# Reordering the first expert's start, the weight conversions and the buffer pools of an attention, expert and gated-MLP kernel

## The chip, the cores and the metric

The kernel runs on one core of a Trainium2 chip. The metric is the time of one execution on the device in microseconds. The engines are TensorE (PE in the rows; PEld is its weight load), VectorE (DVE), ScalarE (ACT), GpSimd (POOL) and SyncE (SP), which issues most transfers.

## The reference

Three layers follow each other; all data are float32 except that the last three matrices are stored as float64 and are read as such by the kernel.

```python
# 1. linear attention: 4 batches, 8 heads, 576 tokens, 64 wide
kv  = einsum('bhsd,bhse->bhde', k, v)
out = einsum('bhsd,bhde->bhse', q, kv)
out = out / sqrt(mean(out * out, -1) + 1e-6) * g_norm      # -> x: 2304 tokens x 512
# 2. experts: 8 of them, each token goes to 2
logits = x @ w_gate + log1p(exp(x @ w_noise)) * noise
top2, weights = two largest, softmax over the two
out[mask] += weight * (relu(x[mask] @ w1[e]) @ w2[e])      # w1 512x1024, w2 1024x512
# 3. gated MLP, 2304 tokens, 512 -> 1536 -> 512
gate = 1 / (1 + exp(-(x @ w_gate)))
out  = (gate * (x @ w_val)) @ w_out
```

## The kernel before

Every product of float32 is made of three products of halves: a high half `h` that PE's number format holds and the low half `l` that is left (high by high, high by low, low by high). ScalarE makes a high half (`activation(hi, raw, Copy)`), VectorE the low half (a subtraction of `hi` from `raw`).

The work comes in stages. **Attention** runs over 18 token tiles of 128; `attend` writes rows to `xbuf` in HBM and `route(g)`, a generator that `advance` steps on, makes ranks and lists for four groups of tiles: its steps on VectorE give the mask `mk`, PE turns it into ranks `prk`, and VectorE makes one-hot rows `ohv`, from which PE makes the lists `lsa` (the first two blocks of expert 0) and `lsb` (all others). **Experts**: GpSimd gathers an expert's tokens by such a list (`gather`), the rows are scaled (`scale`: `xs`), turned on PE (`pxT`) and split into `xh` and `xl` (`expert_in`). Expert 0 starts on its first two blocks before all ranks are known: `h_first(fp, 0)` makes four products `ph`, 24 matmuls each, that `h_out` turns into `ha`; then come `y_step`s (`py`), the second part of expert 0, and experts 1 to 7, each with eight `h_step`s (`ph`, then `hh` on ScalarE and `hl` on VectorE) and five `y_step`s, whose rows go to `ybuf`. **The gated MLP** gathers each token's two rows (`fetch`: `yg`), scales and adds them (`combine`), turns them (`turn`: `px`), and makes the first two tiles in 12 units (`first_unit`: `pgv`) while the others are prepared (`x_parts`); the other 16 tiles take 84 products by a seven-product scheme, whose weight sums `ws` are made beforehand, and the output matrix ends it.

Weights come in units. `tasks` is a list of them in order: an expert's four parts of `w1` and of `w2`, and among them, from the 17th unit on, the parts of the three last matrices, one for every 2.8 units. `load_piece` loads the next raw part into one of four buffers as one comes free; `work` does the next task, and `pump(t)` after each PE step calls it as a planner's credit, free places and expected loads allow. A part of `wg`, `wv` or `wo` is turned from float64 in six VectorE instructions for each of its two halves (`from_double`). A `wo` part is stored to `obuf` and gives its place back; `wg` and `wv` are stored to `wbuf` and keep theirs until `first_weights` splits them in the gated stage. There are 28 places in all; a split part of an expert takes two.

The order on SP and GpSimd is that of the program throughout, on ScalarE nearly so, on VectorE from the second part of expert 0 on, on PE from the last down products on; elsewhere a scheduler orders by priority and its own estimate. `behind(x)` holds GpSimd's queue until `x` is written, by a copy to `seen`. PSUM has eight banks: `psP` has two buffers of two banks and `psA` four of one.

## Time and profile before

| | |
|---|---|
| runs | 953.31, 954.02, 956.75 us; median 954.02 |
| profiled execution | 954.98 us; span of its instructions 953.2 us |
| mean granted TensorE clock | 0.984 |
| busy | PE 919.9 us, PEld 795.6, DVE 690.0, ACT 439.1, POOL 380.9 |
| DMA | 213.93 MB, mean 224 GB/s |

Busy time is that in which an engine works on an instruction; the weight load overlaps the products. The granted clock is a share of full speed, 2.4 GHz; its two levels here are 1.0 and 0.5.

### The profile page before, as it was taken

The numbers are of one execution on the slowest core, as the hardware profiler recorded it, in microseconds if no ns is written. First come the engines' busy times: TensorE is split into PE (matmuls) and PEld (weight loads), VectorE is DVE, ScalarE is ACT, GpSimd is POOL, SyncE is SP. The second block draws the span as 40 slices with busy tenths as digits, with TensorE's granted clock in tenths as the row PEclk, the third lists the DMA queues.
The fourth block names the chain that finished last, engine by engine and source line by source line (L and its number), as shares of the span: only waits on it lengthen the run. The fifth ranks groups of instructions, "written<-read, shape, count | busy, mean of one in ns | idle before, by whom it ended". The sixth has DMA issues, their size and how long they took to land.

```text
span 953.2 us, 14355 instructions
## 1 busy us (share of the span) xinstructions
PE 919.9 (97%) x5155; PEld 795.6 (83%) x5155; DVE 690.0 (72%) x1033; ACT 439.1 (46%) x659; POOL 380.9 (40%) x369
## 2 busy tenths in 40 slices
PE   7987999999999999999999989999999999999998
PEld 4876889889897988979889889888788888888886
DVE  1488688859877595987876458897977876876463
ACT  1674354434343333343343657655555455554441
POOL 2141474737475473736600363242254636300000
PEclk8997999999999999999999989999999999999999
DMA  9995578868776365675753466798477767986784
GB/s 263 281 279 167 189 238 290 282 228 302 256 242 203 112 212 175 211 243 150 243 175 107 131 193 195 230 292 284 143 244 264 264 225 266 343 286 199 221 249 99
DMA packets 134380, 213.93 MB, mean 224 GB/s; under 512 B 20384, under 2 KB 65952, under 8 KB 134304
## 3 DMA queue, kind: packets, MB, share of 16 engines
q1 hardware_dynamic: 122128, 190.05, 61.5%
q0 software_dynamic: 7664, 20.26, 7.4%
q10 hardware_dynamic: 4512, 2.66, 1.0%
q8 instruction: 41, 0.67, 0.3%
q14 instruction: 35, 0.29, 0.1%
HBM read 140.94 MB, written 71.97 MB: 223 GB/s over the span
## 4 chain that ended last, share of the span: by engine, by line
PE 57%; DVE 8%; DMA 3%; issue 3%; ACT 1%; DVEq 0%; SPq 0%; ACTq 0%
PE pga L1163 12%; PE py L806 11%; PE poa L1342 7%; PE ph L762 6%; PE pgc L1163 6%; PE pgv L1131 4%; PE poc L1342 3%; PE pgb L1163 3%; PE pout L1312 2%; PE pob L1342 2%; DVE hl L768 1%; DMA raw<-in_moe_w_dram 1%; DVE raw L611 1%; DMA raw<-in_moe_w_val_dram 1%; ACT hh L767 1%
## 5 line engine op out<-in xcount | busy, mean ns | idle before, releaser
L703 POOL DMA_INDIRECT xg<-xbuf,lsq x132 | 152.4, 1154 | 55.9 <-issue 32.5
L983 DVE TENSOR_TENSOR wt<-lw,wt 128x512 fp32r<-128x512 f32 x84 | 70.9, 850 | 33.2 <-ACT wt L982 27.3
L767 ACT ACTIVATE hh<-ph 128x624 fp32r<-128x624 f32 (+1 forms) x60 | 41.6, 697 | 97.7 <-PE ph L762 74.1
L768 DVE SCALAR_TENSOR_TENSOR hl<-ph,hh 128x624 fp32r<-128x624 f32 (+1 forms) x60 | 48.7, 811 | 52.1 <-ACT hh L767 47.1
L703 POOL DMA_INDIRECT yg<-ybuf,slot x36 | 39.5, 1096 | 83.8 <-DMA ybuf<-yo 44.2
L752 ACT ACTIVATE xh<-xT 128x512 fp32r<-128x512 f32 (+3 forms) x40 | 21.1, 544 | 77.3 <-DVE xT L749 73.5
L722 POOL TENSOR_TENSOR xg<-xg 128x512 f32<-128x512 f32 x33 | 36.7, 1115 | 39.9 <-DMA xg<-xbuf,lsq 39.6
L982 ACT ACTIVATE wt<-lw 128x512 fp32r<-128x512 f32 x84 | 49.8, 621 | 0.3 <-DMA lw<-wbuf 0.2
L1200 POOL TENSOR_TENSOR qt<-qv 128x512 f32<-128x512 f32 x12 | 18.9, 1579 | 69.7 <-DVE qv L1187 27.7
L684 POOL COPY seen<-hh 128x1 f32<-128x1 f32 x42 | 19.4, 462 | 65.5 <-ACT hh L767 64.6
L1177 ACT ACTIVATE q<-pga 128x1024 f32<-128x1024 f32 x24 | 24.7, 1027 | 42.7 <-PE pga L1163 39.6
L811 ACT ACTIVATE yo<-py 128x512 f32<-128x512 f32 (+1 forms) x40 | 23.6, 591 | 42.9 <-PE py L806 37.4
L762 PE MATMUL ph<-xl,w_0h 128*128 128x312 f32 (+2 forms) x128 | 40.2, 314 | 2.4 <-DVE xl L753 2.4
L753 DVE TENSOR_TENSOR xl<-xT,xh 128x512 fp32r<-128x512 f32 (+3 forms) x40 | 25.2, 641 | 23.8 <-ACT xh L752 23.8
L1131 PE MATMUL pgv<-x0h,w 128*128 128x256 f32 x192 | 39.2, 297 | 3.3 <-issue 2.5
L762 PE MATMUL ph<-xh,w_0h 128*128 128x312 f32 (+2 forms) x128 | 40.2, 315 | 1.0 <-ACT xh L752 0.9
L762 PE MATMUL ph<-xh,w_2h 128*128 128x312 f32 (+2 forms) x128 | 39.7, 310 | 1.0 <-DVE hl L768 1.0
L762 PE MATMUL ph<-xh,w_0l 128*128 128x312 f32 (+2 forms) x128 | 39.8, 311 | 0.3 <-PEq L841 0.3
L762 PE MATMUL ph<-xh,w_3h 128*128 128x312 f32 (+2 forms) x128 | 39.3, 307 | 0.3 <-DVE hl L768 0.3
L762 PE MATMUL ph<-xh,w_3l 128*128 128x312 f32 (+2 forms) x128 | 39.3, 307 | 0.0
L762 PE MATMUL ph<-xh,w_1h 128*128 128x312 f32 (+2 forms) x128 | 39.3, 307 | 0.0
L762 PE MATMUL ph<-xh,w_2l 128*128 128x312 f32 (+2 forms) x128 | 39.2, 306 | 0.1
(559 smaller groups left out, 3134.1 us busy)
## 6 DMA issues: line engine op xcount, KB each, us to landing
raw<-in_moe_w_dram SPq DMA_DIRECT2D x60, 512.0 KB
lw<-wbuf SPq DMA_DIRECT2D x84, 256.0 KB
gr<-qbuf SPq DMA_DIRECT2D x42, 512.0 KB
ybuf<-yo SPq DMA_DIRECT2D x32, 256.0 KB
ybuf<-zero SPq DMA_DIRECT2D x29, 256.0 KB
raw<-in_moe_w_gate_dram SPq DMA_DIRECT2D x12, 512.0 KB
raw<-in_moe_w_val_dram SPq DMA_DIRECT2D x12, 512.0 KB
raw<-in_moe_w_out_dram SPq DMA_DIRECT2D x12, 512.0 KB
```

Of the source, the lines that this page charges most:

```text
L703: nc.gpsimd.indirect_dma_start(out=x, out_offset=None, in_=src, in_offset=bass.IndirectOffsetOnAxis(ap=ix, axis=0))
L722: eng.tensor_mul(xv, xv, x[:, :, 128:, None].to_broadcast([128, 4, KD, 32]))
L753: nc.vector.tensor_sub(XL[e, s][:, :, a:z], pt[:, :, o:o + z - a], XA[e, s][:, :, a:z].bitcast(FT))
L762: nc.tensor.matmul(ph, w[:, c, j], x[e, s][:, c, :], start=(n == 0), stop=(n == 3 * KD - 1))
L767: nc.scalar.activation(hh, ph, AF.Relu)
L768: nc.vector.scalar_tensor_tensor(hl, ph, 0.0, hh.bitcast(FT), op0=OP.max, op1=OP.subtract)
L806: nc.tensor.matmul(py[0:m], x[:, f % 2, t], w[:, f % 2, :], start=(n == 0), stop=(n == 3 * FC - 1))
L982: nc.scalar.activation(hi, src, AF.Copy)
L983: nc.vector.tensor_sub(lo, src, hi.bitcast(FT))
L1131: nc.tensor.matmul(pg[:, k // 2, 0:PC], w[:, a, d, s], X0[x][:, 2 * (k % 2) + d, :], start=(k % 2 == 0 and d + a + x == 0), stop=(k % 2 == ...
L1163: nc.tensor.matmul(ps[:, j, 0:HT[c]], w[:, a, k, s], x[:, k, :], start=(first and i == 0), stop=(i == 5), skip_group_check=not first)
L1342: nc.tensor.matmul(ps[:, j, 0:HT[c]], w, g[x][1][:, f, :], start=(first and u + f + i == 0), stop=(u == FP3 - 1 and f + i == 3), skip_grou ...
```

## The change

In the start of expert 0, `work(lows)` puts off the low halves of the first two `w1` parts, with the load behind each. After the scaling of the first two blocks comes the first low half, then the turning and splitting of the tokens, then the first product in three passes (high by high, low weights, low tokens) with steps of the ranks and the second low half between them; DVE and PE keep this order. One of two `advance` steps ahead of it moves behind it. In the task list the six parts of `wo` come first, then `wg` and `wv`, and the last down products pump conversions as others do. From expert 1 on the PSUM pools are made anew: three double-bank buffers for `ph`, two for `py`; a new pool's tile waits for the tiles whose space it takes. In the gated stage the gathers of tiles 5 to 9 go out one by one, each behind a unit's product, and combine, turn and the x parts are put to other steps; so are the gathers of tiles 10 to 13.

```diff
@@ -61,7 +61,7 @@
 PLACES = 11
-FETCHES = {10: 7, 11: 8, 12: 10, 13: 12, 14: 18, 15: 22, 16: 26, 17: 30}
+FETCHES = {10: 9, 11: 10, 12: 12, 13: 13, 14: 18, 15: 22, 16: 26, 17: 30}
 OUT_LOADS = 6
@@ -133,8 +133,9 @@
     gp = moe.enter_context(tc.tile_pool(name="gp", bufs=GBUFS))
-    psP = moe.enter_context(tc.tile_pool(name="psP", bufs=2, space=bass.MemoryType.PSUM))
-    psA = moe.enter_context(tc.tile_pool(name="psA", bufs=4, space=bass.MemoryType.PSUM))
+    banks = moe.enter_context(ExitStack())
+    psP = banks.enter_context(tc.tile_pool(name="psP", bufs=2, space=bass.MemoryType.PSUM))
+    psA = banks.enter_context(tc.tile_pool(name="psA", bufs=4, space=bass.MemoryType.PSUM))
 
@@ -560,7 +561,7 @@
         units += [("w1", e, i) for i in range(FP)] + [("w2", e, i) for i in range(FP)]
-    m2 = [(n, 0, i) for i in range(FP2) for n in ("wg", "wv")] + [("wo", 0, i) for i in range(FP2)]
+    m2 = [("wo", 0, i) for i in range(FP2)] + [(n, 0, i) for i in range(FP2) for n in ("wg", "wv")]
 
@@ -614,7 +615,7 @@
 
-    def work():
+    def work(lows=None):
 
@@ -629,13 +630,19 @@
             wst[u], places[u] = (hi, lo), (i, j)
-            if u[0] == "w1":
-                nc.scalar.activation(hi, raw, AF.Copy, scale=gcol)
-                nc.vector.scalar_tensor_tensor(lo, raw, gcol, hi.bitcast(FT), op0=OP.mult, op1=OP.subtract)
+            nc.scalar.activation(hi, raw, AF.Copy, **({"scale": gcol} if u[0] == "w1" else {}))
+
+            def low():
+                if u[0] == "w1":
+                    nc.vector.scalar_tensor_tensor(lo, raw, gcol, hi.bitcast(FT), op0=OP.mult, op1=OP.subtract)
+                else:
+                    nc.vector.tensor_sub(lo, raw, hi.bitcast(FT))
+                load_piece()
+
+            if lows is None:
+                low()
             else:
-                nc.scalar.activation(hi, raw, AF.Copy)
-                nc.vector.tensor_sub(lo, raw, hi.bitcast(FT))
-            load_piece()
+                lows.append(low)
         elif u[0] == "ws":
@@ -778,7 +785,7 @@
 
-    def h_first(fp, s):
+    def h_first(fp, s, between=None):
 
@@ -788,8 +795,17 @@
         ph = pp([128, 2, 512], "ph")
-        for j in range(2):
-            h_half(ph[:, j, 0:n], 0, 2 * fp + j, s)
+        if between:
+            hi, lo = wst["w1", 0, fp]
+            for k, (w, x) in enumerate(((hi, XA), (lo, XA), (hi, XL))):
+                for j in range(2):
+                    for c in range(KD):
+                        nc.tensor.matmul(ph[:, j, 0:n], w[:, c, j * 128:(j + 1) * 128], x[0, s][:, c, :],
+                                         start=(k + c == 0), stop=(k == 2 and c == KD - 1))
+                between(k)
+        else:
+            for j in range(2):
+                h_half(ph[:, j, 0:n], 0, 2 * fp + j, s)
         h_out(ph[:, :, 0:n], *out)
@@ -934,16 +950,20 @@
 
-    def fetch(t):
+    def fetch(t, js=(0, 1)):
         rows = (t + 1) * E * 128 if t < NB else (NB * E + OVB) * 128
+        if not js[0]:
+            fetch_place(t)
+        for j in js:
+            yg = YG[t][j]
+            rows_of(yg.rearrange("p b w -> p (b w)"), ybuf[0:rows, :], slot[:, t, j:j + 1])
+
+    def fetch_place(t):
         if t < NB - 1:
...
             YG[t] = [y[:, 0], y[:, 1]]
-        for j in range(2):
-            yg = YG[t][j]
-            rows_of(yg.rearrange("p b w -> p (b w)"), ybuf[0:rows, :], slot[:, t, j:j + 1])
 
@@ -989,7 +1009,7 @@
         x = YG.pop(t)
-        pt = pa([128, KD, 128], "px2T")
+        pt = pp([128, 2, 512], "px2T")[:, 0].rearrange("p (c j) -> p c j", c=KD)
         for d in range(KD):
@@ -1439,6 +1459,7 @@
         q_transpose(0)
+    lows = []
     for t in range(NT):
@@ -1452,7 +1473,7 @@
         if t >= FIRST_SPLIT:
-            work()
+            work(lows)
         list_first()
@@ -1461,18 +1482,27 @@
         list_first()
-    advance(2)
-    with in_order("DVE"):
+    advance(1)
+    with in_order("DVE PE"):
         with tc.high_priority():
...
                 scale(0, blk, nc.vector)
-        advance(1)
+        lows[0]()
         with tc.high_priority():
...
                 expert_in(0, blk)
+
+        def ranks_between(k):
+            if k:
+                advance(1)
+            if k == 1:
+                lows[1]()
+
+        h_first(0, 0, ranks_between)
         advance(4)
     for fp in range(FP):
-        h_first(fp, 0)
+        if fp:
+            h_first(fp, 0)
         if fp < 3:
@@ -1527,6 +1557,10 @@
         last = e == E - 1
+        if e == 1:
+            banks.close()
+            psA = moe.enter_context(tc.tile_pool(name="psY", bufs=2, space=bass.MemoryType.PSUM, reuse_waits="tile"))
+            psP = moe.enter_context(tc.tile_pool(name="psH", bufs=3, space=bass.MemoryType.PSUM, reuse_waits="tile"))
         order = ExitStack()
@@ -1596,7 +1630,7 @@
         fetch(blk)
-        pump(0)
+        pump(5.45)
         if 1 <= blk <= EARLY:
@@ -1609,12 +1643,11 @@
 
-    psG = ctx.enter_context(tc.tile_pool(name="psG", bufs=4, space=bass.MemoryType.PSUM))
-    lw = ctx.enter_context(tc.tile_pool(name="lw", bufs=LOADS - AHEAD + 2))
-    g4 = ctx.enter_context(tc.tile_pool(name="g4", bufs=PLACES))
+    psG = ctx.enter_context(tc.tile_pool(name="psG", bufs=4, space=bass.MemoryType.PSUM, reuse_waits="tile"))
+    lw = ctx.enter_context(tc.tile_pool(name="lw", bufs=LOADS - AHEAD + 2, reuse_waits="tile"))
+    g4 = ctx.enter_context(tc.tile_pool(name="g4", bufs=PLACES, reuse_waits="tile"))
     extra.extend(range(PLACES))
-    for t in range(NB - 1, NB + 1):
-        fetch(t)
+    fetch(NB - 1)
 
@@ -1640,20 +1673,25 @@
 
-    def fetch_behind(t):
-
-        behind(Q["first", firsts[now[0] - 1][0]][1][:, firsts[now[0] - 1][1], 0:1])
-        fetch(t)
-
-    for t in range(NB + 1, WHOLE):
-        on(t - NB, fetch_behind, t)
+    def fetch_behind(t, j):
+
+        p, i = firsts[now[0] - 1]
+        behind(Q["first", p][1][:, i, 0:1])
+        fetch(t, (j,))
+
     for t in range(PLAIN, WHOLE):
-        on(t - PLAIN, combine, t)
-        on(t, turn, t)
+        k = t - PLAIN
+        if t >= NB:
+            for j in range(2):
+                k = -(-(2 * (t - NB) + j + 1) * 2 // 3)
+                on(k, fetch_behind, t, j)
+            k += 1
+        on(k, combine, t)
+        on(k + PLAIN, turn, t)
     for t in range(WHOLE, NT):
...
     first_parts = x_parts(0)
-    for k in (6, 7, 9, 9, 9, 10, 10):
+    for k in (7, 8, 10, 10, 10, 11, 11):
         on(k, first_parts.pop(0)[2])
```

## Rows read from the trace of the kernel before

**Rows 1.** The page: the span, and busy time of TensorE (PE).

```profile
span 953.2 us, 14355 instructions
...
PE 919.9 (97%) x5155; PEld 795.6 (83%) x5155; DVE 690.0 (72%) x1033; ACT 439.1 (46%) x659; POOL 380.9 (40%) x369
```

**Rows 2.** PE's waits over the span: who for; us, times, longest us.

```profile
PE prk L486 <- DVE mk L481: 4.2, 2, 3.7
PE pgv L1131 <- issue: 2.9, 6, 1.0
...
PE py L806 <- DVE hl L768: 2.0, 1, 2.0
PE py L806 <- DVE w_3l L637: 1.9, 1, 1.9
...
PE ph L762 <- DVE hl L768: 1.3, 4, 0.3
...
PE pgv L1131 <- ACT yo L811: 0.7, 1, 0.7
```

**Rows 3.** Windows of PE: stretch, length, busy (instructions), granted clock, DMA share, GB/s.

```profile
76.00:78.00 2.00, 0.71 (x5) 0.50 0.82 187
...
294.00:296.00 2.00, 2.00 (x7) 0.60 0.81 251
296.00:298.00 2.00, 2.00 (x7) 0.55 0.15 30
...
408.00:410.00 2.00, 2.00 (x6) 0.50 0.73 248
...
562.00:564.00 2.00, 1.39 (x7) 0.50 0.48 131
```

**Rows 4.** Timeline of PE, start of expert 0: start, us, instruction, [idle before, releaser].

```profile
77.29 0.19 PE L486 MATMUL prk<-mk,tri 128*128 128x40 bf16 x1 [3.65 <-DVE mk L481]
...
82.67 0.58 PE L762 MATMUL ph<-xl,w_0h 128*128 128x256 f32 x1 [1.92 <-DVE xl L753]
...
96.34 0.63 PE L806 MATMUL py<-w_0h,ha 128*128 128x512 f32 x2
```

**Rows 5.** Timeline of VectorE (DVE), 60 to 112 us.

```profile
72.15 1.28 DVE L634 SCALAR_TENSOR_TENSOR w_0l<-raw,gcol,w_0h 128x1024 fp32r<-128x1024 f32 x1
...
75.55 1.29 DVE L709 TENSOR_TENSOR xs<-xg 128x512 f32<-128x512 f32 x2
...
79.47 0.24 DVE L509 TENSOR_TENSOR ohr<-oh,prk 128x80 f32<-128x80 f32 x1 [1.77 <-PE prk L492]
...
87.89 0.69 DVE L768 SCALAR_TENSOR_TENSOR ha<-ph,ha 128x512 fp32r<-128x512 f32 x1 [0.55 <-ACT ha L767]
88.93 1.29 DVE L634 SCALAR_TENSOR_TENSOR w_2l<-raw,gcol,w_2h 128x1024 fp32r<-128x1024 f32 x1 [0.35 <-ACT w_2h L633]
...
100.15 0.19 DVE L1488 TENSOR_SCALAR lsb<-plist 128x40 int32<-128x40 f32 x1
```

**Rows 6.** The chain that ended last: one unit of the gated stage.

```profile
570.34 2.88 PE pgv L1131 x24
```

**Rows 7.** Timeline of DVE in expert 5.

```profile
377.02 0.81 DVE L768 SCALAR_TENSOR_TENSOR hl<-ph,hh 128x624 fp32r<-128x624 f32 x1 [7.16 <-ACT hh L767]
...
405.25 1.21 DVE L637 TENSOR_TENSOR w_3l<-raw,w_3h 128x1024 fp32r<-128x1024 f32 x1
```

**Rows 8.** Timeline of ScalarE (ACT) in expert 3.

```profile
285.84 0.66 ACT L604 ACTIVATE wv<-raw 128x512 f32<-128x512 f32 x1 [2.00 <-DMA raw<-in_moe_w_val_dram]
```

**Rows 9.** Windows of all engines: busy PE, PEld, DVE, ACT, POOL; clock, DMA.

```profile
500.00:550.00 50.00, 49.31 (x284) 43.78 (x283) 29.08 (x45) 24.58 (x41) 9.18 (x10) 1.00 0.38 117
```

**Rows 10.** Timeline of PE, fifth unit of the gated stage and what follows.

```profile
557.09 0.28 PE L1131 MATMUL pgv<-x0h,w 128*128 128x256 f32 x1 [0.17 <-issue]
...
565.54 1.06 PE L1029 MATMUL px<-ident,x 128*128 128x128 f32 x4
```

**Rows 11.** Timeline of ACT in the same stage.

```profile
553.77 0.72 ACT L951 ACTIVATE yg<-yg,tw 128x512 f32<-128x512 f32 x1 [1.18 <-DMA yg<-ybuf,slot]
```

## The prediction

> **What bounds the kernel.** I read the page's busy times first: TensorE (PE) is busy 919.9 of 953.2 us [rows 1], so in most of the span one of its products ends last and no edit off PE shortens it. The change touches the number of products nowhere. What can be gained is PE's idle time and the time in which its products run at the low clock, so I read PE's waits next [rows 2] and then PE's busy time and granted clock by stretches [rows 3]. Four places matter.
>
> First, the start of expert 0: the rank product `prk` waits (3.65 us of its 4.2 stand at 77.29 us [rows 4]), then the first product waits 1.92 us at 82.67 for the low tokens `xl`, and from 76 us on the granted clock is 0.50, that is 1.2 of 2.4 GHz. Second, PE stops in the down products of two experts, 2.0 us for `hl` and 1.9 us for `w_3l`, and the clock is at or near 0.50 for some 3.4 us behind each [rows 2, 3]. Third, the h products wait four times, 1.3 us in all, for a PSUM buffer that `hl` still reads. Fourth, in the first units of the gated stage PE shows gaps of 2.9 us with no releaser (`issue`), again with the low clock behind them [rows 2, 3].
>
> **1. First tokens ahead of low halves and ranks.** Now DVE makes a low half of `w1` at 72.15 and another after it (1.28 us each), then scales the tokens at 75.55 without idle before it [rows 5]: it was free late, not the gather. The rank product, queued ahead of the token transposes on PE, waits for DVE's `mk`. The change takes 2.56 us of DVE work from ahead of the scaling, and puts both the transposes and eight products that need only `w_0h` and `xh` ahead of the ranks. So PE starts expert 0 earlier: the gathers land by my estimate at 73 to 74 us, then two scalings (1.29), transposes, the copies to `xh`, and the first products at about 76.4 us where the full stream now starts at 82.67 [rows 4].
>
> But this gain mostly isn't kept. DVE does the same list of work until `w_2l` is done (88.93 + 1.29 = 90.2 us), and then until the list `lsb` at 100.15, which the next three gathers need. Between 72 and 90 us it idles 1.77 (for `prk`), 0.55 (for `ha`) and 0.35 us [rows 5], 2.7 in all. That is what a better order can give the third product; the order itself removes no DVE instruction. Against it stands new waiting: the second scaling may wait for its gather, and in the fixed order the ranks behind it wait too. The two raw loads that follow a low half go out later with it (SP stands behind them with the row stores of group 3, which now start at 81 us anyway); their weights are used after 93 us, so that costs nothing. Bounds: -4 (the idle goes, and half of the 2.6 us of low halves comes out of the path) and +3 (below). I take half of 2.7: **-1.3**.
>
> Here PE will sit idle in a new place. 48 products at the full rate (24 in 2.88 us, [rows 6]) end near 82 us, and `w_2l` comes near 88. A stop of 3.65 us was followed by 0.50 [rows 3, 4]. The Trainium skill (TensorE: Matmul & The Clock Gate, "HAM oscillation — how this bites in real kernels") says that an array left waiting between bursts goes back to the slow clock and starts each burst cold; the trace agrees with 0.50 behind the stop. It speaks against this part, since the next burst would start cold; by it the sum is the clock rival's below, 948.9 us, without it 944.6.
>
> **2. Out matrix first.** The twelve `wg`/`wv` each hold one of 28 weight places from conversion to the end; an expert's halves hold 16. From expert 5 on all 28 are taken, so splits wait for a place, then bunch. The rows show it: DVE idles 7.16 us before 377.02, then works with hardly a break until `w_3l` at 405.25, which PE waits for [rows 7]. In expert 3 ScalarE waits 2.00 us for a raw load at 285.84, with `hh` behind it in its order [rows 8]; that makes `hl` late for PE. The `wo` matrices give their place back at once, so with them first both causes go: at expert 5 six `wg`/`wv` are held instead of eleven or twelve. Same conversions, same stores; the twelve half-sums and their stores move from experts 2 to 5 to experts 4 to 7. Prices: the stops 2.0 + 1.9, and half of about 3.4 us of low clock behind each, 1.7 each: 7.3 us. A loading wait like that at 285.84 can come back elsewhere, so I take **-6.0**; bounds -7.3 and +3.7 (one stall more).
>
> `pump(5.45)` lets conversions run in the last down products. DVE is busy 29.08 of 50 us from 500 to 550 [rows 9], so 20.9 us are free; the last value matrix and its sums fit. Cost nothing.
>
> **3. PSUM pools from expert 1.** Three double-bank buffers for h instead of two: the 1.3 us of waits on `hl` [rows 2] go, of which I take **-1.0**. Two buffers for `py` suffice while ScalarE reads one out during the next block. The first new tile may wait for an eviction of the old pool, as `pgv` does for `yo` (0.7, [rows 2]): **+0.2**, bounds 0 and 0.7. The token transposes use an h buffer, free by then. That first wait of `pgv` stays, for its banks may still be those of `py`.
>
> **4. First units.** One unit is 24 products, 2.88 us [rows 6]; the fifth goes from 557.09 to 565.54, 8.45 us, some 5.6 too long, with the clock at 0.50 from 562 on [rows 3, 10]. With the rest of the slow time about 6.8 us. PE waits there for no data that the trace shows. It lies in a run of gathers issued back to back by GpSimd; the change spaces them, one and a half to a unit and each behind a product. A later run of gathers passes without a stop, so the gathers alone don't explain it. Bounds 0 and -6.8; I take a bit under half, **-3.0**. Against it: the combine of tiles 8 and 9 and the x parts come one step later, where DVE is nearly full: +0 to +2, I take **+0.7**. A tile's second gather now goes out one unit ahead of its scaling, and the next sigmoid is queued behind that scaling on ScalarE, then PE's PSUM tile behind the sigmoid; ScalarE waits 1.18 us for a gather at 553.77 already [rows 11], without a stop of PE at that point. If it came to that in each of five tiles it is 5.9 us on ScalarE, of which PE's four PSUM tiles cover at least a unit (2.88) each time; I add nothing. The ten `seen` copies (six more) are on GpSimd, idle otherwise. FETCHES come later, but long before use: nothing.
>
> **Sum.** -1.3 - 6.0 - 1.0 + 0.2 - 3.0 + 0.7 = -10.4 us. The profiled execution took 954.98 us (span 953.2, 1.8 around it), 0.96 above the median 954.02 of the runs. 954.98 - 10.4 = 944.6 us. A difference under 0.5% (4.8 us) can't be told from none.
>
> **Rivals.**
> *The clock eats the first stage.* PE stands from about 82 to 88 us, the last two of the four first products (48 matmuls) run at half rate throughout, 11.5 instead of 5.8 us from 88, and the down products start at 99.5 and not at 96.34 [rows 4]. Then part 1 is +3, not -1.3: 948.9 us. For it: 0.50 behind 3.65 us [rows 3, 4]. Against it: DVE's order might bring `w_2l` earlier. Chance 0.14. The page named in part 1 states this rule.
>
> *The stalls only move.* Places were not the cause, raw loads were [rows 8], and two stops return in other experts: part 2 gives 0, 950.6 us. Chance 0.13, within the 0.5%.
>
> *All ends come true*: -2.7 - 7.3 - 1.3 - 6.8: 936.9 us. Chance 0.13.
>
> *Slower.* In the last expert 16 places of halves and 12 of gate and value make 28 again. If splits wait there until the first `w1` comes back, the rest of the conversions piles up in DVE's fixed order ahead of the first weights and the adds that PE's next transposes need. Part 2 then gives 0 (950.6 us) and PE stops as long as the pile exceeds the 20.9 free us; from a stop of 4.4 us on the kernel is slower, and 10 us make 960.6 us. For it: DVE ran 28 us with hardly a break in expert 5 [rows 7]. Against it: no next expert's tokens there. Chance 0.06.
>
> **Chances.** My forecast 0.54, rivals as above (0.46 with them). Faster by over 0.5%: nearly all of the forecast, the clock rival and the good ends, 0.77; same 0.15; slower 0.08. The likeliest case's own range is 939 to 949 us; over all 8 in 10 it is 935.5 to 951.5, from the good end to past the moved stalls.
>
> **What would show it.** Right: scalings ahead of `w_0l`; first h products near 76.4 us; no wait of `py` over 0.5 us; held places no longer stopping the splits; the fifth unit under 4 us. Wrong: PE idle over 4 us before `w_2l`; `py` waits for `w_3l` or `hl` anew; PE waits for `xs` at the first gated products, one step late; the gap in the units unchanged. The sum fails most where the gap of unknown cause stays or goes whole (3 us either way).

## The result, and the profile after

The changed kernel is slower: 961.36 us against 954.11 (medians of 22 runs each, on one chip), ratio 1.0066, 95% interval 1.0054 to 1.0077. 944.6 had been forecast. Its profiled execution took 960.72 us. The page gives its span and PE's busy time:

```profile
span 958.7 us, 14349 instructions
...
PE 919.9 (96%) x5153; PEld 794.5 (83%) x5155; DVE 680.4 (71%) x1033; ACT 438.0 (46%) x659; POOL 382.0 (40%) x375
```

PE is busy as long as before, to the tenth [rows 1]; all 5.5 us of longer span are waiting. PE's waits (engine, line and tile waited for; us in total, times, longest):

```profile
PE pxT L752 <- DVE xs L716: 4.3, 3, 1.8
PE ph L769 <- DVE oh L474: 3.7, 1, 3.7
...
PE ph L769 <- ACT xh L759: 2.6, 4, 1.2
PE px L1049 <- issue: 2.3, 1, 2.3
...
PE pga L1183 <- ACT q L1197: 2.1, 1, 2.1
PE ph L769 <- DVE hl L775: 1.8, 2, 0.9
```

Against [rows 2], the stops of `py` for `hl` and `w_3l` are gone, as are most of the gaps of `pgv` (0.8 us are left). The waits of `ph` for `hl` are not gone: they are two and not four, but 1.8 us instead of 1.3, both in experts 1 and 2. Beside them PE waits for token rows (`xs`) of expert 0's second part, for `xh` at the start of an expert, at a turn (`px`) and at the first products of the scheme.

Where the time went is read from starts in PE's timeline. Expert 0's first product is 3.5 us earlier than before (76.42 us), its first down product 1.0 later, its second part 4.5 later, expert 1 6.0 later. Experts 1 to 7 give 2.4 back, the gated units 1.7; from the first product of the scheme on 3.7 are lost. That is 6.0 - 2.4 - 1.7 + 3.7 = 5.6 us.

VectorE around the list `lsb` (start, us, instruction, [idle before, releaser]; here and below, lines are left out between):

```profile
80.24 0.24 DVE L510 TENSOR_TENSOR ohr<-oh,prk 128x80 f32<-128x80 f32 x1 [1.28 <-PE prk L493]
...
82.99 1.28 DVE L637 SCALAR_TENSOR_TENSOR w_2l<-raw,gcol,w_2h 128x1024 fp32r<-128x1024 f32 x1 [0.23 <-ACT w_2h L633]
...
97.56 0.24 DVE L510 TENSOR_TENSOR ohr<-oh,prk 128x80 f32<-128x80 f32 x1 [2.32 <-PE prk L493]
...
98.98 1.22 DVE L639 TENSOR_TENSOR w_1l<-raw,w_1h 128x1024 fp32r<-128x1024 f32 x1
...
102.31 1.22 DVE L639 TENSOR_TENSOR w_2l<-raw,w_2h 128x1024 fp32r<-128x1024 f32 x1
...
103.93 1.22 DVE L639 TENSOR_TENSOR w_3l<-raw,w_3h 128x1024 fp32r<-128x1024 f32 x1
105.06 0.19 DVE L1518 TENSOR_SCALAR lsb<-plist 128x40 int32<-128x40 f32 x1
...
109.05 0.69 DVE L716 TENSOR_TENSOR xs<-xg 128x512 f32<-128x512 f32 x1 [3.68 <-DMA xg<-xbuf,lsb]
```

PE in the same stretch:

```profile
90.95 0.55 PE L769 MATMUL ph<-xh,w_3h 128*128 128x256 f32 x1 [3.72 <-DVE oh L474]
...
97.14 0.23 PE L487 MATMUL prk<-mk,tri 128*128 128x40 bf16 x1
...
112.13 0.66 PE L752 MATMUL pxT<-ident,xs 128*128 128x128 f32 x4 [1.62 <-DVE xs L716]
114.55 1.09 PE L752 MATMUL pxT<-ident,xs 128*128 128x128 f32 x4 [1.76 <-DVE xs L716]
```

And PE's windows (stretch, length, busy of PE, PEld, DVE, ACT, POOL, granted clock, DMA share, GB/s):

```profile
91.00:97.00 6.00, 5.44 (x24) 5.14 (x24) 4.21 (x15) 1.32 (x3) 0.00 (x0) 0.50 0.32 89
...
114.00:121.00 7.00, 5.98 (x25) 5.71 (x26) 4.67 (x20) 0.54 (x1) 2.84 (x3) 0.52 0.64 217
599.00:602.00 3.00, 3.00 (x9) 2.32 (x8) 2.48 (x4) 3.00 (x5) 0.45 (x1) 0.50 0.80 257
```

In the kernel before, the last ranks and the steps behind them read (one line of PE, then two of VectorE):

```profile
94.15 0.20 PE L486 MATMUL prk<-mk,tri 128*128 128x40 bf16 x1
...
94.53 0.24 DVE L509 TENSOR_TENSOR ohr<-oh,prk 128x80 f32<-128x80 f32 x1
...
95.53 1.22 DVE L637 TENSOR_TENSOR w_0l<-raw,w_0h 128x1024 fp32r<-128x1024 f32 x1
```

So `lsb` comes at 105.06 and not at 100.15 [rows 5]. PE stops 3.72 us ahead of the fourth product, runs that product's 24 matmuls at 0.50 until 97.34, and only then makes the last ranks `prk`, at 97.14 instead of among the matmuls of that product; VectorE waits 2.32 us for them. Behind that, three low halves of `w2` stand between these ranks and `lsb`; in the kernel before it was one (`w_0l`), and the others came after `lsb`. The gathers, the rows `xs`, PE's transposes and a second stretch at 0.52 follow.

### The profile page after: what moved, and what is told of

Same layout as the page of the kernel before. It is cut to its first block, busy times and chain, and to the rows that moved or that the text cites. A ratio compares the mean times of both kernels' runs of the same rounds, so it can differ in the third digit from the quotient of the medians.

```text
span 958.7 us, 14349 instructions
## 1 busy us (share of the span) xinstructions
PE 919.9 (96%) x5153; PEld 794.5 (83%) x5155; DVE 680.4 (71%) x1033; ACT 438.0 (46%) x659; POOL 382.0 (40%) x375
## 5 line engine op out<-in xcount | busy, mean ns | idle before, releaser
L775 DVE SCALAR_TENSOR_TENSOR hl<-ph,hh 128x624 fp32r<-128x624 f32 (+1 forms) x60 | 48.7, 812 | 56.8 <-ACT hh L774 48.0
L710 POOL DMA_INDIRECT yg<-ybuf,slot x36 | 38.6, 1071 | 81.4 <-DMA ybuf<-yo 51.0
L759 ACT ACTIVATE xh<-xT 128x512 fp32r<-128x512 f32 (+3 forms) x40 | 21.1, 544 | 83.5 <-DVE xT L756 79.1
L1002 ACT ACTIVATE wt<-lw 128x512 fp32r<-128x512 f32 x84 | 49.7, 620 | 0.0
L769 PE MATMUL ph<-xh,w_0h 128*128 128x312 f32 (+1 forms) x120 | 38.2, 318 | 2.6 <-ACT xh L759 2.6
L769 PE MATMUL ph<-xl,w_3h 128*128 128x312 f32 (+2 forms) x128 | 40.2, 314 | 0.0
L769 PE MATMUL ph<-xl,w_2h 128*128 128x312 f32 (+2 forms) x128 | 39.1, 306 | 0.0
L769 PE MATMUL ph<-xh,w_1l 128*128 128x312 f32 (+2 forms) x128 | 39.1, 306 | 0.0
```

The costliest lines, as they stand in the source:

```text
L710: nc.gpsimd.indirect_dma_start(out=x, out_offset=None, in_=src, in_offset=bass.IndirectOffsetOnAxis(ap=ix, axis=0))
L769: nc.tensor.matmul(ph, w[:, c, j], x[e, s][:, c, :], start=(n == 0), stop=(n == 3 * KD - 1))
L775: nc.vector.scalar_tensor_tensor(hl, ph, 0.0, hh.bitcast(FT), op0=OP.max, op1=OP.subtract)
L1002: nc.scalar.activation(hi, src, AF.Copy)
```

## Experiments

Jobs ran on several chips, on which the kernel before took 945.9 to 954.5 us (medians), so only ratios to the kernel before on the same chip are compared; stage lengths are read in each trace. Theory: the loss is the late list, the pools in expert 1 and the spaced gathers. Rival: the early start itself, by PE's stops and the clock behind them, or a bad phase that spoils the parts that come later.

In the table, "expert 0" is the time from the end of the last attention product `po` to expert 1's first `ph`, "1, 2" and "3-7" the experts up to the first `pgv`, "units" from there to the first `pga`, "rest" to the end of the span; `lsb` and the second part's first `ph` (368 columns) are starts. All us.

| kernel | ratio (95%) | lsb | second part | expert 0 | 1, 2 | 3-7 | units | rest |
|---|---|---|---|---|---|---|---|---|
| before (first profile) | | 100.1 | 111.8 | 76.4 | 111.3 | 285.9 | 44.9 | 364.4 |
| before_again | | 98.8 | 110.5 | 75.7 | 111.4 | 284.8 | 44.9 | 364.4 |
| changed | 1.0066 (1.0054-1.0077) | 105.1 | 116.3 | 82.6 | 116.1 | 278.6 | 43.2 | 368.2 |
| after_again | 1.0094 (1.0072-1.0116) | 104.0 | 115.1 | 81.2 | 117.1 | 281.0 | 44.3 | 363.8 |
| start_alone | 1.007 (1.0051-1.009) | 107.0 | 118.2 | 82.2 | 111.7 | 284.0 | 38.4 | 364.4 |
| start_undone | 1.0046 (1.0026-1.0066) | 98.8 | 110.6 | 75.6 | 118.3 | 277.5 | 43.1 | 363.8 |
| units_undone | 1.0048 (1.0031-1.0065) | 105.3 | 116.4 | 80.7 | 116.8 | 279.3 | 38.1 | 364.4 |
| out_first_alone | 0.9979 (0.9963-0.9994) | 100.4 | 112.2 | 76.8 | 111.3 | 281.8 | 38.5 | 364.4 |
| start_w3_early | 1.0004 (0.9979-1.003) | 100.1 | 112.1 | 77.5 | 112.1 | 282.9 | 48.7 | 364.4 |
| start_ranks_first | 1.004 (1.0009-1.0072) | 101.4 | 112.4 | 79.1 | 111.6 | 288.1 | 49.7 | 364.4 |
| start_lists_ahead | 1.0025 (1.0006-1.0045) | 100.2 | 113.0 | 77.6 | 111.8 | 282.3 | 38.9 | 364.4 |
| pools_alone | 0.9984 (0.9961-1.0006) | 99.7 | 111.2 | 76.6 | 113.5 | 280.0 | 49.4 | 364.4 |
| out_pools_late | 0.9969 (0.9945-0.9992) | 100.4 | 112.4 | 77.0 | 111.9 | 279.8 | 44.1 | 364.4 |
| out_pools_at_2 | 0.995 (0.993-0.9971) | 100.6 | 112.1 | 77.3 | 112.6 | 278.5 | 39.0 | 364.4 |
| out_units | 0.9988 (0.9967-1.001) | 100.3 | 111.8 | 76.5 | 111.6 | 281.4 | 49.5 | 363.8 |
| out_units_pairs | 0.9958 (0.9937-0.998) | 99.8 | 111.3 | 76.6 | 111.8 | 280.8 | 42.9 | 368.6 |
| best1 | 0.9992 (0.9969-1.0015) | 102.4 | 113.6 | 79.3 | 112.9 | 278.0 | 46.2 | 364.4 |
| best2 | 0.9967 (0.9951-0.9982) | 100.6 | 113.6 | 79.5 | 112.3 | 277.3 | 38.6 | 364.4 |

### The parts alone and undone

**start_alone**: the kernel before with the hunks of the start (`lows`, `h_first` in passes, the fixed order).

```diff
-            work()
+            work(lows)
...
-    advance(2)
-    with in_order("DVE"):
+    advance(1)
+    with in_order("DVE PE"):
...
+        h_first(0, 0, ranks_between)
```

> The kernel before with part 1 of the change alone (first tokens ahead of the low halves and ranks, first product in passes, fixed order of VectorE and PE in that stretch). In the changed kernel PE is 3.6 us ahead of the old one at the first h product and 6.0 us behind it at 132 us. Theory: this edit alone does that and nothing later takes it back, so 954 + 6 = 960 us, ratio 1.006, with lsb near 105 us and a stop of PE of 3 to 4 us ahead of the first product with w_3h. Rival: the experts are paced by raw loads and places, which swallow the delay within an expert or two: 954 to 956 us, ratio at most 1.002, although lsb is as late.

Measured 1.007: the theory. Expert 0 is 5.8 us longer than in the kernel before's first profile, 5.4 and 6.6 us longer than in out_first_alone and start_undone, which have the old start on the same chip, and nothing later takes that back.

**start_undone**: the changed kernel with those hunks taken out.

```diff
-            work(lows)
+            work()
...
-    with in_order("DVE PE"):
+    with in_order("DVE"):
```

> The changed kernel with the start of expert 0 as before; parts 2 to 4 stay. Theory: the 6.0 us come back, 961.4 - 6 = 955 us, ratio to before 0.999 to 1.002, so parts 2 to 4 together are worth almost nothing. Rival (my prediction's parts 2 to 4 were right and only met a bad phase behind a late start): the stage of the experts gains its 5 to 7 us and the gated stage its 2 to 3, 945 to 948 us, ratio 0.992.

Measured 1.0046, worse than either said. The start is as before, yet experts 1 and 2 take 7 us longer and, beside out_first_alone on the same chip, the units 4.6; experts 3 to 7 win 4.3. So the start is not all of it.

**out_first_alone**: part 2 on the kernel before.

```diff
-    m2 = [(n, 0, i) for i in range(FP2) for n in ("wg", "wv")] + [("wo", 0, i) for i in range(FP2)]
+    m2 = [("wo", 0, i) for i in range(FP2)] + [(n, 0, i) for i in range(FP2) for n in ("wg", "wv")]
...
-        pump(0)
+        pump(5.45)
```

> The kernel before with part 2 alone: the wo matrices converted first, and conversions pumped in the last down products. Theory: the two stops of py for hl and w_3l (3.9 us and some 3.4 us of low clock) go, and PE's new short waits in expert 1 and 2 for tokens and weights (about 3 us in the changed kernel) come: 954 - 7.3 + 3 = 950 us, ratio 0.995. Rival: the stops went for another reason (three h buffers, or the shift by 6 us): then they stand, 954 to 957 us.

Measured 0.9979, faster, but by 2 us and not by 4 or more. Both stops of `py` are gone; one stop is new, in expert 5. ScalarE:

```profile
387.58 0.66 ACT L604 ACTIVATE wg<-raw 128x512 f32<-128x512 f32 x1 [5.63 <-DMA raw<-in_moe_w_gate_dram]
388.14 0.67 ACT L767 ACTIVATE hh<-ph 128x624 fp32r<-128x624 f32 x1
```

and PE:

```profile
389.71 0.41 PE L762 MATMUL ph<-xh,w_2h 128*128 128x312 f32 x1 [2.24 <-DVE hl L768]
```

This is the wait of [rows 8] again, a raw load with `hh` queued behind it on ScalarE, now where two buffers for `ph` are too few. Experts 1 and 2 don't pay, so the short waits there in the changed kernel are not from the `wo` order alone.

**units_undone**: the changed kernel with the units' hunks taken out.

```diff
+    for t in range(NB + 1, WHOLE):
+        on(t - NB, fetch_behind, t)
     for t in range(PLAIN, WHOLE):
...
+        on(t - PLAIN, combine, t)
+        on(t, turn, t)
...
-    for k in (7, 8, 10, 10, 10, 11, 11):
+    for k in (6, 7, 9, 9, 9, 10, 10):
```

> The changed kernel with the first units as before (gathers of tiles 5 to 9 two at a time, combine, turn, x parts and later gathers at the old steps). Theory: the stop of PE for xs_6l at the first gated products (2.1 us and 3.4 us of low clock) goes, the gaps of the fifth unit with their low clock return, as do the waits saved there: from the first products to the end 3.6 us are won and 1.7 lost ahead of them, 961.4 - 1.9 = 959.5 us, ratio to before 1.0055. Rival: the gap of the fifth unit hung on when gathers and conversions met and does not return: 957.5 us, ratio 1.0035.

Measured 1.0048; the ratios of theory and rival both lie near it. The stages decide: units 38.1 us, where start_undone with the new ones takes 43.1, and the rest 364.4. The gap of the fifth unit does not return. On this chip the old units are the fast ones.

### What makes the list late

**start_w3_early**: start_alone, with two more conversions ahead of the rank steps.

```diff
         h_first(0, 0, ranks_between)
+        work()
+        work()
         advance(4)
...
-        if fp < 3:
+        if fp == 2:
             work()
```

> Part 1 alone (as start_alone, ratio 1.007), with the third and fourth part of w1 converted ahead of the four rank steps that follow the first product, so that ScalarE makes w_3h ahead of the rank activations it waits in. Theory: in the changed kernel the stop of 3.7 us ahead of the product with w_3h and the low clock behind it put that product's end and the rank product behind it at 97 us, which is half of why lsb comes 4.9 us late; the other half are low halves of w2 that VectorE makes ahead of the last steps of the list. So the stop and the low clock go, the list comes 2 to 3 us earlier, and the ratio falls to 1.003 to 1.005. Rival 1: the stop is all of it: ratio 1.000. Rival 2: the order of VectorE alone sets lsb, and the stop was free waiting: ratio stays at 1.007.

Measured 1.0004. PE's stop ahead of the fourth product became longer, and the clock fell behind it all the same, but the ranks went between the matmuls:

```profile
91.29 0.58 PE L768 MATMUL ph<-xh,w_3h 128*128 128x256 f32 x1 [5.04 <-DVE ha L774]
...
94.24 0.26 PE L486 MATMUL prk<-mk,tri 128*128 128x40 bf16 x1
```

and on VectorE the list came as early as before:

```profile
94.71 0.24 DVE L509 TENSOR_TENSOR ohr<-oh,prk 128x80 f32<-128x80 f32 x1
...
100.08 0.19 DVE L1515 TENSOR_SCALAR lsb<-plist 128x40 int32<-128x40 f32 x1
```

So my theory that the stop was half of the loss falls in that form, and so does rival 1: with 5.0 us of stop the ratio is 1.0004, and expert 0 takes 77.5 us, where nine traces with the old start show 75.6 to 77.3. Rival 2 is right that the stop is free, but its 1.007 did not come. What counts is when `lsb` comes, and here both halves of its delay are gone: the ranks stand among the matmuls (`ohr` at 94.71), and one low half, `w_1l`, stands between them and `lsb`, not three. This run does not part the two.

The stop did not go, since PE did not wait for `w_3h` here. ScalarE had made that by 83.03 us, and the row of the stop names `ha`: `psP` has two buffers, and VectorE's step that frees the second product's ends at 91.23. In the changed kernel `w_3h` and this `ha` both end at 90.80, so its trace does not part them. ScalarE, then VectorE:

```profile
81.89 1.14 ACT L632 ACTIVATE w_3h<-raw,gcol 128x1024 fp32r<-128x1024 f32 x1
...
90.56 0.67 DVE L774 SCALAR_TENSOR_TENSOR ha<-ph,ha 128x512 fp32r<-128x512 f32 x1
```

**start_ranks_first**: start_alone, with the second product ahead of the next conversion in the fixed order, and four more rank steps behind that conversion.

```diff
         h_first(0, 0, ranks_between)
         advance(4)
+        h_first(1, 0)
+        work()
+        advance(4)
...
-        if fp:
+        if fp > 1:
             h_first(fp, 0)
-        if fp < 3:
+        if 0 < fp < 3:
             work()
```

> Part 1 alone as in start_alone (ratio 1.007), but in the fixed order four more rank steps of the last group stand ahead of the low halves of the third and fourth part of w1, and the second product ahead of them. In start_w3_early PE stopped 5.0 us ahead of the fourth product and the kernel was as fast as before, with lsb at 100.1 us as before and not at 105.1. Theory: lsb alone sets when the second part of expert 0 starts (some 11.5 us behind it in each trace), PE's stops ahead of it are free. With the mask of the last group ready 2 to 3 us earlier, lsb comes near 97 to 98 us, the second part near 109, and the ratio is 0.997 to 0.998. Rival: the early second part then waits for PE, which has its down products still to do: second part not ahead of 111 us, ratio 1.000.

A miss: 1.004. The low halves of the third and fourth part of `w1` still ran ahead of the last group's mask, but the mask came at 91.09 us, where it is 94.60 in the changed kernel, and its product with it (PE, then VectorE):

```profile
92.95 0.19 PE L486 MATMUL prk<-mk,tri 128*128 128x40 bf16 x1
...
93.55 0.23 DVE L509 TENSOR_TENSOR ohr<-oh,prk 128x80 f32<-128x80 f32 x1
```

Yet `lsb` came at 101.4, 7.8 us behind `ohr`, with three low halves of `w2` between them as in the changed kernel. So early ranks alone don't make the list early; VectorE's order behind them is the other half. The second part is 11.0 us behind `lsb`, near the 11.5 that were said.

**start_lists_ahead**: start_w3_early, with the last steps written ahead of the down products, in VectorE's fixed order.

```diff
+    with in_order("DVE"):
+        while routes:
+            advance(1)
...
     for blk in range(AB):
-        y_step(0, blk, lambda f: advance(1))
+        y_step(0, blk)
```

> As start_w3_early (lsb at 100.1 us, second part at 112.1, ratio 1.000), with the last list written ahead of the down products in the program and VectorE kept in that order there, so that the low half w_1l of w2 (1.2 us) stands behind lsb. Theory: lsb comes 1.2 us earlier and the second part with it, the first down products wait for w_1l for nothing: second part 11 to 12 us behind lsb as in nine traces so far, ratio 0.998 to 0.999. Rival: the down products, begun later, become what is late: second part more than 12.5 us behind lsb, ratio 1.000 or more.

The rival's numbers: 1.0025, second part 12.7 us behind `lsb`. Its cause is not what the trace shows, for the last of the three `xs` waits for its gather:

```profile
110.33 0.69 DVE L715 TENSOR_TENSOR xs<-xg 128x512 f32<-128x512 f32 x1 [2.59 <-DMA xg<-xbuf,lsb]
```

Counted from the end of attention the list is 0.8 us earlier than in start_w3_early (28.7 for 29.5), and expert 0 is as long (77.6 for 77.5). An earlier list no longer brings the tokens earlier there; why the gather is slower is not shown.

### The pools

**pools_alone**: part 3 on the kernel before.

```diff
+        if e == 1:
+            banks.close()
+            psA = moe.enter_context(tc.tile_pool(name="psY", bufs=2, ...
+            psP = moe.enter_context(tc.tile_pool(name="psH", bufs=3, ...
```

> Part 3 alone, the new PSUM pools from expert 1 on. Theory: experts 1 and 2 take 116 us or more where they took 111.3, PE waiting for xh at the second column half of expert 1's first product and for weights behind it; the later experts win about 2 us on their waits for h buffers, while the two stops of py for hl and w_3l stay, as the wo matrices are not first: ratio 1.002 to 1.004. Rival: with conversions in the old order the loss in expert 1 doesn't come (it was from the wo conversions, whose VectorE work stands ahead of the tokens): ratio 0.998.

Measured 0.9984, the rival's ratio, though part of the theory's loss comes: experts 1 and 2 take 2.2 us longer. Experts 3 to 7 gain 5, and one of the two stops of `py`, that for `hl`, is gone as well.

**out_pools_late** and **out_pools_at_2**: parts 2 and 3, with the new pools ahead of expert 3, and of expert 2.

```diff
-        if e == 1:
+        if e == 3:
```

```diff
-        if e == 1:
+        if e == 2:
```

> Parts 2 and 3, start and units as before, but the new PSUM pools are made ahead of expert 3 and not of expert 1. With the pools from expert 1 on, experts 1 and 2 took 116 to 118 us together, without them 111.3; experts 3 to 7 took 277.5 to 279.3 with them and 281.7 without. Theory 1: the cost belongs to expert 1, where the two spare buffers for py and turned tokens are wanted and tokens come late, and the gain to the later experts: 111 + 279 us, some 3 us less than part 2 alone, ratio 0.994 to 0.996. Theory 2: the swap itself costs 4 to 5 us wherever it stands, as the first tiles wait for the old ones: expert 3 takes 60 instead of 55 us, ratio 1.000.

> Parts 2 and 3 with the new pools made ahead of expert 2 (out_pools_late made them ahead of expert 3, ratio 0.997; the change ahead of expert 1, where experts 1 and 2 together took 5 to 7 us more). Theory: in expert 1 PE's order around the first product changes with the pools, so that it asks for the last tokens after 12 matmuls instead of 18, and waits 1.0 to 1.7 us for them with the low clock behind; expert 2's tokens lie ready, so pools made there cost nothing: experts 1 and 2 at 111 to 112 us, ratio 0.995 to 0.998. Rival: the first expert with new pools always pays as long as PE's order is the scheduler's: expert 2 at 58 us or more, ratio 1.000 or more.

Measured 0.9969 and 0.995, the lowest ratio here; experts 1 and 2 at 111.9 and 112.6 us. The swap costs little by itself; made at expert 1 it does. PE's timeline in the changed kernel:

```profile
155.70 0.41 PE L769 MATMUL ph<-xh,w_0h 128*128 128x312 f32 x1 [1.19 <-ACT xh L759]
```

and with part 2 alone:

```profile
150.28 0.56 PE L762 MATMUL ph<-xh,w_0h 128*128 128x312 f32 x2 [0.49 <-ACT xh L752]
```

The tokens are as late in both, 3.1 and 3.2 us after the expert's first matmul. But PE, in the scheduler's order there, has 18 matmuls to do ahead of them in the kernels with the old pools in expert 1, and 12 in all that make them new there. In start_undone a wait of 1.32 us and 3.4 us at 0.50 follow. That this order comes from the pools is shown; that it is all of the 5 to 7 us is not. The same order costs pools_alone 2.2 us; with `wo` first beside it, in start_undone, PE waits in experts 1 and 2 for `hh`, `hl` and `yo` too, 0.4 to 0.7 us each, which pools_alone does not show.

### The gathers of the units

**before_again**: the kernel before, unchanged.

```diff
 (no line differs)
```

> The kernel before, unchanged, once more with a profile. In its first profile the stage of the gated units (first pgv to first product of the scheme) took 44.9 us, with gaps without a releaser in the fifth unit and 6.8 us at half clock. In the runs of start_alone, out_first_alone and units_undone, which leave that stage as it was, it took 38.1 to 39.1 us without these gaps, and the kernel before was 8 us faster beside them. Theory: the gap of the fifth unit belongs to an execution or a chip, not to the kernel, and is absent here: about 946 us, units 38 to 39 us. Rival: it is the kernel's, and the changes elsewhere moved it away: units near 45 us.

The units took 44.9 us again, with gaps that have no releaser, now at other places. PE's waits:

```profile
PE px L1029 <- issue: 1.6, 2, 0.9
...
PE pgv L1131 <- issue: 1.2, 3, 0.6
```

On the chips of start_alone and of best2, the old units have no such gap in any of six traces (with changes elsewhere) and take 38.1 to 39.0 us; on the chips of this run and of pools_alone the old units show 1.2 us or more of such gaps of `pgv` in all six traces and take 44.1 to 49.7 us. So the gaps went with the chip here, or with the job that ran on it; the runs can't tell the two apart. That bears out the first half of my theory, but the gaps are not absent in this run, and they were not moved away by the changes elsewhere, as the rival had it.

**out_units** and **out_units_pairs**: parts 2 and 4; and the same with both gathers of a tile at the step of the first.

```diff
             for j in range(2):
...
-                on(k, fetch_behind, t, j)
+                if not j:
+                    on(k, fetch_behind, t)
```

> The kernel before with parts 2 and 4 (wo first, conversions in the last down products, first units with spaced gathers and later steps), start and pools as before. Beside it stands out_first_alone, which is part 2 alone: ratio 0.998, units 38.4 us. Theory: the spaced gathers make ScalarE wait 2 to 3 us for the second gather of a tile, the combine behind it comes late, PE waits some 2.6 us at a turn and runs 3.4 us at half clock: units 43 us, so 4.5 us more than part 2 alone, ratio 1.002 to 1.003. Rival: the later units of the changed kernel are slow because of its pools (px turned from another pool, banks waited for), not because of the gathers: units 38 to 39 us, ratio 0.998.

> As out_units, but both gathers of a tile go out together, at the step of the first: the second one 1 step (a unit, 2.9 us) earlier for most tiles, the combine where it was. In out_units and the changed kernel ScalarE waited 2 to 3 us for the second gather of a tile, which goes out one step ahead of its scaling. Theory: these waits fall under 1 us, the turn no longer waits, and the stage of the units falls by about 2 to 3 us (on a chip without the gaps that have no releaser, from 43 to 40 us). Rival: what waits is GpSimd itself, held by the product it must come behind: units as in out_units.

Measured 0.9988 and 0.9958, on two chips that both show the gaps; the intervals overlap. out_units has 3.2 us of gaps of `pgv`, so spacing the gathers does not remove them. ScalarE's wait for gathers from 540 to 600 us is 7.4 to 9.3 us in the four traces with part 4, 6.4 with pairs, and 0.7 to 5.9 with the old gathers; the longest single wait is 2.8 to 3.3, 2.6, and at most 1.6. So the waits don't fall under 1 us as I had said, and that pairs are faster is not shown. The turn's wait of 2.5 us comes in out_units without the new pools, so the pools, which the rival blamed, are not its cause.

**after_again**: the changed kernel, beside out_pools_at_2 and best2 on a chip without the gaps.

> The changed kernel once more, beside the next three and with the kernel before on the same chip. Its first comparison gave 1.0066. Theory (the loss sits in the start, expert 1 and the gated units, and does not hang on the chip): 1.005 to 1.009, expert 0's second part some 4.5 us late, experts 1 and 2 at 116 us together. Rival: on this chip the gaps without a releaser in the units decide and the ratio falls under 1.003 or rises over 1.010.

Measured 1.0094, just above the theory's 1.009, which the interval covers: units 44.3 us beside 39.0. Waits from 540 to 600 us in it:

```profile
ACT yg L971 <- DMA yg<-ybuf,slot: 9.3, 8, 3.3
...
PE px L1049 <- DVE xf L1058: 3.5, 2, 2.6
```

and in out_pools_at_2, with the old gathers:

```profile
ACT yg L952 <- DMA yg<-ybuf,slot: 3.7, 6, 1.2
...
PE px L1030 <- DVE xf L1039: 0.7, 1, 0.7
```

A tile's second gather goes out one step ahead of its scaling. ScalarE waits for it, the copy of the last turn out of PSUM (`xf`) is queued behind, and PE's next turn waits for that copy. The wait of `px` without a releaser in the changed kernel's first profile (2.3 us) is the same one, for PE starts as the copy ends:

```profile
582.64 0.42 DVE L1058 COPY xf<-px 128x256 f32<-128x256 f32 x1
...
583.11 0.66 PE L1049 MATMUL px<-ident,x 128*128 128x128 f32 x4 [2.34 <-issue]
```

One stop of that first profile is absent here, with a rest of 363.8:

```profile
598.61 0.51 PE L1183 MATMUL pga<-xs_6h,wt 128*128 128x512 f32 x1 [2.07 <-ACT q L1197]
```

The low clock of 599 to 602 follows it. Of the five traces with the new units' steps two have it, this profile and out_units_pairs, so it belongs to single executions.

### What held, put together

**best1** and **best2**: parts 2 and 3 with the pools from expert 3, with the start of start_ranks_first and of start_lists_ahead.

```diff
-        if e == 1:
+        if e == 3:
...
+        h_first(1, 0)
+        work()
+        advance(4)
```

```diff
-        if e == 1:
+        if e == 3:
...
+        work()
+        work()
         advance(4)
...
+    with in_order("DVE"):
+        while routes:
```

> Parts 2 and 3 with the pools from expert 3 on (ratio 0.997), and the start of start_ranks_first; first units as before. If the gains add, 0.997 times 0.9975, 0.994 to 0.995. If the start gains nothing, 0.997. If the early start makes tokens of expert 1 late for its h products again, 1.000 or more.

> Parts 2 and 3 with the pools from expert 3 on, and the start of start_lists_ahead; first units as before. If the two add: 0.997 times 0.9985, 0.995 to 0.996. If the short stops of PE at the turned tokens and the low clock behind them eat the start's gain: 0.997 to 0.999.

Measured 0.9992 and 0.9967: no form of the new start is shown to add to what parts 2 and 3 give. Of the versions that beat both kernels out_pools_at_2 has the lowest ratio: old start, old units, `wo` first, pools from expert 2, 0.995. Its interval (0.993 to 0.9971) overlaps those of out_first_alone, out_pools_late and best2, so that it is the best of them is not shown.

## Why the prediction was wrong

By stages of the two first profiles the forecast was -1.3 us for expert 0, +0.2 for experts 1 and 2, -7.0 for experts 3 to 7, -2.3 for the units and nothing for the rest. Measured were +6.1, +4.8, -7.3, -1.7 and +3.7. So the sum failed at the start, at the swap of the pools and behind the gathers; that the late experts and the units come near is partly luck, since the late experts' gain was split wrongly between parts 2 and 3, and the units' hung on gaps that other chips don't show.

**Part 1** was the step that failed most: -1.3 us forecast, +5.8 measured (start_alone), outside its bounds of -4 and +3. The text had the right limit, the list `lsb` at 100.15, but then credited half of VectorE's idle time to it, as if the order of all else would stay. It did not: the last rank product moved behind PE's fourth product (+3.0 us at `ohr`, 97.56 for 94.53) and two more low halves moved in between (+1.9 from `ohr` to `lsb`, 7.5 for 5.6 us). That makes the 4.9 us; from the second part to expert 1 it is 36.4 us instead of 34.9, with the second stretch at half clock. In all traces but the two with the list written ahead (12.7 and 13.0), the second part starts 11.0 to 12.0 us behind `lsb`, wherever PE stood before it.

**The clock rival** named a real event with the wrong price. The stop (3.72 us, forecast as 6) was followed by 0.50, and the Trainium skill (TensorE: Matmul & The Clock Gate, "HAM oscillation — how this bites in real kernels"), by which an array left waiting starts its next burst cold, agrees with it. But start_w3_early stops longer, falls to 0.50 as well, and is as fast as before. The place was wrong too: `w_2l` was made at 82.99 and not near 88 us, the third product ran without a stop, and PE stood ahead of the fourth.

**Part 2** was right in its mechanism and too large: -6.0 forecast, about -2 in time and -3 to -4 in experts 3 to 7. The rival "the stalls only move" was partly true: in out_first_alone a raw load on ScalarE stopped PE in expert 5.

**Part 3** was mis-sized both ways: the gain in the late experts is about 5 us alone (I took 1.0, from the waits of `ph` for `hl`; but the stop of `py` for `hl`, which I had counted under part 2, goes with part 3 alone too), the cost at the swap 2 to 7 us in experts 1 and 2 (I took 0.2, from a single wait for PSUM). PE's order there was not in my sum.

**Part 4**: the gap of the fifth unit went (that unit takes 3.1 us), but it was not the gathers' distance that made it: the old gathers run without the gap on two chips. The ScalarE wait that the text described and priced at nothing ("I add nothing") is what the stage now pays, 7.4 to 9.3 us on ScalarE and 2.3 to 3.5 on PE at a turn: the units end 1.7 us better on the first chip, and 5.3 worse beside out_pools_at_2.

Of the signs: first products at 76.4 us, scalings ahead of `w_0l` and no long wait of `py` came true; PE's wait one step late at the first gated products came as a wrong sign. The last-expert pile of the rival "slower" did not: PE's first wait there is 0.69 us, as before.

## What to carry to other kernels

Moving work ahead of a chain helps only if the chain's own instructions keep their places: before costing idle time as a gain, list on each engine what will stand ahead of the chain's next step in the new order. Here a stop of PE ahead of a late list was free (5.0 us, ratio 1.0004); an instruction of that list behind a burst of products was not (3.0 us). A new buffer pool changed the scheduler's order here, so look at the first tiles after the swap, and leave a gather at least the steps that its old lead had.

## What was unexpected of the hardware

The units of the kernel before took 44.9 us in two traces, with PE gaps that nothing releases (`issue`), while kernels with the same units took 38.1 to 39.0 us on two other chips without them: about as large a difference as the change's own effect. Whether the chip or the job on it brings the gaps, and what causes them, stays open; no run here was made for it.
